# A decode block's output projection and FFN2 with activations stationary in column tiles

## The chip, the cores and the metric

One core of one Trainium2 chip runs the whole program. The metric is device time in microseconds (us) of one execution; most executions of one kernel agree within a few tenths of a microsecond, and "span" is the profiled execution from its first to its last instruction. In this text PE is TensorE (PEld its weight loads), DVE is VectorE, ACT is ScalarE, POOL is GpSimd and SP is SyncE, the engine that issues all large loads here. The page counts 16 DMA engines to the core, and the trace has 16 landings for each of the 73 large loads; I take these shares as one an engine.

## The reference

Two parallel branches share a layer-normalised token, two batch rows, one new position each:

```python
xn = layernorm(x)                                      # x: [2, 1, 512]
q = (xn @ wq)                                          # 32 heads of 128
o = softmax(q . K / sqrt(128)) . V                     # K, V: [2, 32, 8192, 128] bf16
out = x + o @ wo + relu(xn @ w1) @ w2                  # wo: [4096, 512], w1: [512, 1792]
```

K and V are 134 MB each, so nearly all of the work is reading them once.

## The kernel before

The parts that the change and the argument touch, cut. The head of PE's program, with the small FFN done while the first K tile is under way:

```python
for j in range(FJ):                                    # FJ = 14, after FFN1 and relu
    i = pe.matmul(y, lhsT=hT[:, j, :], rhs=w2_sb[:, j, :],       # [128x2] stationary, 512 moving
                  start=(j == 0), stop=(j == FJ - 1))
...
v.tensor_tensor(out=ys[:], in0=y, in1=xsb[:], op=ALU.add)        # DVE: FFN + x, [2, 512]
...
with pe.Fori(...):            # the loop over 32 tiles of K and V: transposes, scores, weighted sums
```

The tail, after the loop. The last V tile comes in two halves, wo in five pieces of 14, 7, 6, 3 and 2 of 32 slices:

```python
for k in range(KT):                                    # KT = 4: FFN + x transposed into fin, f32
    pe.matmul(fin[:, k, :], lhsT=ys[:, k * P:(k + 1) * P], rhs=ident2[:], start=(k == 0), stop=False)
...                                                    # last weighted sum, heads to OX
for c in range(NC):
    pe.wait_ge(dW[c], 16)                              # piece c of wo has landed
    for j in range(cuts[c], cuts[c + 1]):
        for k in range(KT):
            t = pe.matmul(fin[:, k, :], lhsT=wo_sb[:, j, k * P:(k + 1) * P], rhs=OX[:, j, :], ...)
...
v.tensor_copy(yT[:], fin...)                           # DVE, then
pe.transpose(tp[1][0:8, 0, :], yT[...], identb[:])     # PE, then
v.tensor_copy(osb[:], tp[1][0:8, 0, :])                # DVE
sp.dma_start(out.rearrange("b s (c p) -> (b s c) p", p=P), osb[:])   # 8 neighbouring partitions
```

## Time and profile before

| | before |
|---|---|
| time, first three runs | 660.88 us median (660.88 to 661.12) |
| span of the profiled execution | 658.7 us |
| read from HBM | 280.50 MB, 426 GB/s over the span |
| last piece of wo landed | 654.86 us |
| store issued | 656.09 us |
| store's issue to end of span | 2.57 us |

The prediction below shows the page's lines and the two timelines that matter.

### The profile page before, as it was taken

Reading aid. Unit: us, or ns where it says so; the run is one execution under the profiler, and the core shown is the slowest. Engines: PE = TensorE matmul, PEld = TensorE weight load, DVE = VectorE, ACT = ScalarE, POOL = GpSimd, SP = SyncE. Lnnn points to the kernel's source line nnn. Section 1 sums busy time; section 2 is a strip of 40 time slices with the busy share of each in tenths; the row PEclk is TensorE's granted clock in tenths of the full one; section 3 lists DMA queues with packets and bytes.
Section 4 is the critical chain, followed back from the end, with each engine's and each line's share of the span. In section 5 each row is a group of like instructions: output and inputs, shape, how many; then the busy total and the mean of one; then the engine's idle time right before and its main releaser. Section 6 shows DMA issues by size and latency. Waiting matters only on the chain.

```text
span 658.7 us, 26859 instructions
## 1 busy us (share of the span) xinstructions
PE 559.9 (85%) x12737; PEld 536.7 (81%) x12737; DVE 253.2 (38%) x436; ACT 255.8 (39%) x403; POOL 8.8 (1%) x46
## 2 busy tenths in 40 slices
PE   2897799998889978789878878987888898878897
PEld 0497798987889978789878878987888898878896
DVE  1144344443434434334433434443334443434341
ACT  1034344443433534244353434434343434433340
POOL 1000000000000000000000000000000000000000
PEclk9889999998998989899988989898899988989996
DMA  8999999999999999999999999999999999999996
GB/s 365 433 440 420 439 428 431 436 426 438 422 442 422 440 432 428 438 424 442 420 442 424 436 436 426 438 422 442 424 438 430 430 438 424 440 422 442 424 425 282
DMA packets 10542, 280.66 MB, mean 426 GB/s; under 512 B 1186, under 2 KB 1188, under 8 KB 1700
## 3 DMA queue, kind: packets, MB, share of 16 engines
q1 hardware_dynamic: 10528, 280.50, 99.1%
q8 instruction: 9, 0.15, 0.1%
q14 instruction: 1, 0.01, 0.0%
q10 hardware_dynamic: 4, 0.00, 0.0%
HBM read 280.50 MB, written 0.00 MB: 426 GB/s over the span
## 4 chain that ended last, share of the span: by engine, by line
DMA 58%; PE 37%; ACT 2%; issue 1%; SPq 1%; ACTq 0%; DVE 0%
DMA ks<-in_A_k_cache_dram 54%; PE tp L288 21%; PE Sc L295 11%; PE ot L308 4%; DMA w_sb<-in_A_wo_dram 4%; ACT kT L415 2%; ACT L415 1%; SPq L190 0%; PE Sc L343 0%; SPq L185 0%; PE Sc L346 0%; SPq L173 0%; SPq L172 0%; SPq L166 0%; PE ot L400 0%
## 5 line engine op out<-in xcount | busy, mean ns | idle before, releaser
L288 PE MATMUL tp<-identb,ks 128*128 128x128 bf16 x4096 | 323.4, 228 | 67.8 <-DMA ks<-in_A_k_cache_dram 67.8
L415 DVE COPY kT<-tp 128x1024 bf16<-128x1024 bf16 x320 | 219.7, 691 | 323.8 <-PE tp L288 323.5
L288 PEld LDWEIGHTS tp<-identb,ks 128*128 128x128 bf16 x4096 | 255.0, 102 | 71.6 <-DMA ks<-in_A_k_cache_dram 71.5
L415 ACT COPY kT<-tp 128x1024 bf16<-128x1024 bf16 x192 | 194.3, 1012 | 231.2 <-PE tp L288 231.2
L295 PE MATMUL Sc<-q,kT 128*128 128x64 bf16 x4096 | 217.1, 196 | 9.3 <-ACT kT L415 6.1
L295 PEld LDWEIGHTS Sc<-q,kT 128*128 128x128 bf16 x4096 | 178.8, 100 | 13.1 <-ACT kT L415 9.6
L308 PE MATMUL ot<-prm,vs 128*128 128x64 bf16 x4224 | 157.6, 193 | 3.3 <-issue 3.3
L308 PEld LDWEIGHTS ot<-prm,vs 128*128 128x128 bf16 x4224 | 140.5, 98 | 6.2 <-issue 3.6
L528 ACT COPY nm<-Sc 128x2 f32<-128x2 f32 x32 | 5.1, 160 | 119.8 <-PE Sc L346 119.8
L532 ACT ACTIVATE prm<-Sc,nm 64x128 bf16<-64x128 f32 x64 | 25.7, 401 | 4.4
L469 DVE TENSOR_REDUCE mcol<-Sc 64x1 bf16<-64x128 f32 x64 | 18.6, 291 | 20.0 <-PE Sc L295 19.5
L415 ACT ACT_TABLE_LOAD x16 | 20.5, 1283 | 2.2
L243 PE MATMUL ot<-vs,xz 128*16 128x512 bf16 x32 | 8.6, 436 | 8.1 <-DMA vs<-in_A_wq_dram 8.1
L474 DVE TENSOR_REDUCE mx<-Sc 1x2 bf16<-1x128 bf16 x32 | 8.9, 279 | 16.9 <-PE Sc L343 16.9
L520 ACT COPY OTf<-ot 128x2 f32 x32 | 5.1, 160 | 26.1 <-PE ot L308 26.1
L243 PEld LDWEIGHTS ot<-vs,xz 128*16 128x16 bf16 x32 | 3.1, 99 | 13.1 <-issue 10.4
L228 POOL COPY q<-qb 128x2 bf16<-128x2 bf16 x32 | 5.8, 184 | 590.1 <-PE Sc L295 568.2
L532 ACT ACTIVATION_READ_ACCUMULATOR prm<-Sc,nm x64 | 11.8, 185 | 0.0
L445 DVE TENSOR_SCALAR qs<-ot 16x512 bf16<-16x512 f32 x1 | 0.7, 678 | 16.5 <-PE ot L243 16.5
L343 PE MATMUL Sc<-identb,mcol 128*1 128x128 bf16 x32 | 7.0, 217 | 0.0
L346 PE MATMUL Sc<-mx,onesb 1*128 1x2 bf16 x32 | 5.5, 172 | 0.0
L400 PE MATMUL ot<-OX,w_sb 128*128 128x2 bf16 x128 | 4.0, 166 | 1.1 <-DMA w_sb<-in_A_wo_dram 0.7
(56 smaller groups left out, 38.0 us busy)
## 6 DMA issues: line engine op xcount, KB each, us to landing
ks<-in_A_k_cache_dram SPq DMA_DIRECT2D x32, 4096.0 KB, 26.7
vs<-in_A_v_cache_dram SPq DMA_DIRECT2D x31, 4096.0 KB, 31.3
vs<-in_A_wq_dram SPq DMA_DIRECT2D x1, 4096.0 KB, 12.1
vs<-in_A_v_cache_dram SPq DMA_DIRECT2D x2, 2048.0 KB, 19.0
w_sb<-in_B_w_dram SPq DMA_DIRECT2D x2, 1792.0 KB, 17.9
w_sb<-in_A_wo_dram SPq DMA_DIRECT2D x1, 1792.0 KB, 25.1
w_sb<-in_A_wo_dram SPq DMA_DIRECT2D x1, 896.0 KB, 26.8
w_sb<-in_A_wo_dram SPq DMA_DIRECT2D x1, 768.0 KB, 28.2
```

The costliest lines, as they stand in the source:

```text
L228: g.tensor_copy(q2[t % R][:], qb[:, 2 * t:2 * t + 2]).then_inc(sQ1, 1)
L243: i = pe.matmul(qp, lhsT=xz[:, kt, Z - g * Bsz:Z - g * Bsz + QG * Bsz], rhs=vs[1][:, (kt * QG + g) * 512:(kt * QG + g + 1) * 512], start=( ...
L288: t = pe.transpose(tp[e % 4][:, i, :], ks[r][:, kk * Dh:(kk + 1) * Dh], identb[:])
L295: t = pe.matmul(Sc[r][:, 2 * kk:2 * kk + 2 * REP], lhsT=kT[e % 4][:, i, :], rhs=rep(q2[r][:]), start=True, stop=True,)
L308: t = pe.matmul(ot[r][:, 0:2 * REP], lhsT=vs[r][:, kk * Dh:(kk + 1) * Dh], rhs=rep(prm[r][:, kk, :]), start=(kk == 0), stop=(kk == KB - 1),)
L343: pe.transpose(tr_of(r), mcol[r][:], identb[:]).then_inc(sT, 1)
L346: pe.matmul(bc_of(r), lhsT=onesb[:], rhs=mx[r][:], start=True, stop=True).then_inc(sB, 1)
L415: fn(kT[e % 4][:], tp[e % 4][:]).then_inc(kR[e], 1)
L469: m = v.tensor_reduce(out=mcol[i][half, :], in_=S_of(i)[half, :, u], axis=AX.X, op=ALU.max)
L474: v.tensor_reduce(out=mx[i][:], in_=tr_of(i).rearrange("o (u m) -> o u m", u=2), axis=AX.X, op=ALU.max, negate=True,).then_inc(sX, 1)
L520: a.copy(OTf[:, bass.ds(c, 2)], ot[r][:, 0:2]).then_inc(sO, 1)
L532: x = a.activation(out=prm[i][half, :, u], in_=S_of(i)[half, :, u], func=ACTF.Exp, bias=nm[i][half, u:u + 1], scale=1.0, accum_out=RS[half ...
```

## The change

The intent is a shorter tail. The two activations become the stationary operand, 32 columns wide with the two batch rows in columns 0 and 16 and zeros between, and the weights the moving one. The four column blocks of the result go to four column tiles of the array, partitions 32c to 32c+31. The result is then already in rows, so that one DVE add and one store of eight rows, 16 partitions apart, replace copy, transpose and copy. FFN2 takes the same form so that its rows lie where those of wo do.

```diff
-    y = Sc[1][0:Bsz, :]
-    fin = ot[0][:, 0:KT * Bsz].rearrange("p (b c) -> p c b", c=KT)
+    y = Sc[1][:, 0:P]
+    fin = ot[0][:, 0:P]
+    def cols(ap, c):
+        return ap[c * CT:(c + 1) * CT, :]              # CT = 32, CB = 16
+    def store(eng):
+        eng.dma_start(out.rearrange("b s (c p) -> c (b s) p", p=P),
+                      osb[0:P - CB + 1:CB, :]).then_inc(dO, 16)
...
         for j in range(FJ):
-            i = pe.matmul(y, lhsT=hT[:, j, :], rhs=w2_sb[:, j, :], ...)
+            for c in range(KT):
+                pe.matmul(cols(y, c), lhsT=hT[:, j, :], rhs=w2_sb[:, j, c * P:(c + 1) * P], ...)
+        for c in range(KT):
+            i = pe.matmul(cols(y, c), lhsT=onex[:], rhs=xsb[:, c * P:(c + 1) * P], ...)
...
-        for k in range(KT):
-            pe.matmul(fin[:, k, :], lhsT=ys[:, k * P:(k + 1) * P], rhs=ident2[:], ...)
...
                     t = pe.matmul(
-                        fin[:, k, :], lhsT=wo_sb[:, j, k * P:(k + 1) * P], rhs=OX[:, j, :], ...
+                        cols(fin, k), lhsT=OX[:, j, :], rhs=wo_sb[:, j, k * P:(k + 1) * P], ...
-        pe.transpose(tp[1][0:Bsz * KT, 0, :], yT[:]..., identb[:])
...
-        v.tensor_copy(yT[:], ...)
-        v.tensor_copy(osb[:], tp[1][0:Bsz * KT, 0, :])
+        v.tensor_tensor(out=osb[:], in0=fin, in1=ys[:], op=ALU.add)
```

(Zero fills and semaphore counts are left out.)

More of the change, by code (lines that the diff above doesn't have):

```diff
@@ L59 @@
     eps = 1e-5
+    CT = P // KT
+    CB = CT // Bsz
+    assert KT * Bsz * CB == P
     ctx.enter_context(tc.tile_critical(no_gpsimd_drain=True))
@@ L81 @@
     identb = sb([P, P], bf16, "identb")
-    ident2 = sb([Bsz, Bsz], f32, "ident2")
     sel = sb([H, DQ, P], bf16, "sel")
@@ L107 @@
     Ob = sb([H, Bsz, Dh], bf16, "Ob")
-    OX = sb([P, WJ, Bsz], bf16, "OX")
-    hT = sb([P, FJ, Bsz], bf16, "hT")
-    ys = sb([Bsz, D], f32, "ys")
-    yT = sb([P, Bsz, KT], bf16, "yT")
-    osb = sb([Bsz * KT, P], bf16, "osb")
+    OX = sb([P, WJ, CT], bf16, "OX")
+    hT = sb([P, FJ, CT], bf16, "hT")
+    ys = sb([P, P], f32, "ys")
+    osb = sb([P, P], bf16, "osb")
+    onex = sb([Bsz, CT], bf16, "onex")
     tp = [ps([P, EG, P], bf16, f"tp{i}") for i in range(4)]
@@ L155 @@
     hp = ot[1][:, 0:FJ * Bsz].rearrange("p (j b) -> p j b", b=Bsz)
-    y = Sc[1][0:Bsz, :]
-    fin = ot[0][:, 0:KT * Bsz].rearrange("p (b c) -> p c b", c=KT)
+    y = Sc[1][:, 0:P]
[3 more added lines that the diff above has]
+    def store(eng):
+        eng.dma_start(
+            out.rearrange("b s (c p) -> c (b s) p", p=P),
+            osb[0:P - CB + 1:CB, :],
+        ).then_inc(dO, 16)
     def load_k(t):
@@ L191, in _ @@
         sp.wait_ge(sE, 1)
-        sp.dma_start(
-            out.rearrange("b s (c p) -> (b s c) p", p=P), osb[:]
-        ).then_inc(dO, 16)
+        store(sp)
     @(lambda f: f(nc.gpsimd))
@@ L217, in _ @@
             g.wait_ge(sI, 3 + u)
-        g.memset(ident2[:], 0.0).then_inc(sG, 1)
-        g.wait_ge(sG, 5)
-        g.affine_select(
-            out=ident2[:], in_=ident2[:], compare_op=ALU.not_equal, fill=1.0,
-            base=0, pattern=[[-1, Bsz]], channel_multiplier=1,
-        ).then_inc(sI, 1)
+        g.memset(OX[:], 0.0).then_inc(sI, 1)
         g.wait_ge(sV, 100)
@@ L272, in _ @@
         for j in range(FJ):
-            i = pe.matmul(
-                y,
-                lhsT=hT[:, j, :],
-                rhs=w2_sb[:, j, :],
-                start=(j == 0),
-                stop=(j == FJ - 1),
+            for c in range(KT):
+                pe.matmul(
+                    cols(y, c),
+                    lhsT=hT[:, j, :],
+                    rhs=w2_sb[:, j, c * P:(c + 1) * P],
+                    start=(j == 0),
+                    stop=False,
+                )
+        for c in range(KT):
+            i = pe.matmul(
+                cols(y, c),
+                lhsT=onex[:],
+                rhs=xsb[:, c * P:(c + 1) * P],
+                start=False,
+                stop=True,
             )
@@ L364, in _ @@
         t.then_inc(sH, 1)
-        for k in range(KT):
-            pe.matmul(
-                fin[:, k, :],
-                lhsT=ys[:, k * P:(k + 1) * P],
-                rhs=ident2[:],
-                start=(k == 0),
-                stop=False,
-            )
         for i in range(2):
@@ L400, in _ @@
                     t = pe.matmul(
-                        fin[:, k, :],
-                        lhsT=wo_sb[:, j, k * P:(k + 1) * P],
-                        rhs=OX[:, j, :],
-                        start=False,
-                        stop=(j == WJ - 1 and k == KT - 1),
+                        cols(fin, k),
+                        lhsT=OX[:, j, :],
+                        rhs=wo_sb[:, j, k * P:(k + 1) * P],
+                        start=(j == 0),
+                        stop=(j == WJ - 1),
                     )
         t.then_inc(sH, 1)
-        pe.wait_ge(sV, 106)
-        pe.transpose(
-            tp[1][0:Bsz * KT, 0, :], yT[:].rearrange("p b c -> p (b c)"), identb[:]
-        ).then_inc(sH, 1)
     def kcopy(eng, e):
@@ L422, in _ @@
         v.memset(xz[:], 0.0).then_inc(sZ, 1)
+        v.memset(onex[:], 0.0)
+        v.memset(hT[:], 0.0).then_inc(sZ, 1)
         v.memset(prm[R - 1][:], 0.0).then_inc(sP, 1)
@@ L440, in _ @@
         v.wait_ge(sQ, 1)
+        v.wait_ge(sI, 1)
         v.wait_ge(sZ, 1)
@@ L447, in _ @@
         ).then_inc(sV, 1)
+        v.wait_ge(sZ, 2)
+        v.tensor_copy(onex[:, 0:CT:CB], identb[0:Bsz, 0:Bsz])
         v.wait_ge(sF, 1)
         v.tensor_scalar(
-            out=hT[:], in0=hp, scalar1=0.0, scalar2=None, op0=ALU.max,
+            out=hT[:, :, 0:CT:CB], in0=hp, scalar1=0.0, scalar2=None, op0=ALU.max,
         ).then_inc(sF, 1)
@@ L458, in _ @@
         v.wait_ge(sF, 3)
-        v.tensor_tensor(out=ys[:], in0=y, in1=xsb[:], op=ALU.add).then_inc(sF, 1)
+        v.tensor_copy(ys[:], y).then_inc(sF, 1)
         def pair(i, n):
@@ L500, in _ @@
         v.wait_ge(sH, 3)
+        v.wait_ge(sI, 5)
         v.tensor_copy(
-            OX[:], Sc[1][:, 0:Bsz * WJ].rearrange("p (b j) -> p j b", b=Bsz)
+            OX[:, :, 0:CT:CB], Sc[1][:, 0:Bsz * WJ].rearrange("p (b j) -> p j b", b=Bsz)
         ).then_inc(sV, 1)
         v.wait_ge(sH, 4)
-        v.tensor_copy(yT[:], ot[0][:, 0:KT * Bsz].rearrange("p (b c) -> p b c", c=KT)).then_inc(sV, 1)
-        v.wait_ge(sH, 5)
-        v.tensor_copy(osb[:], tp[1][0:Bsz * KT, 0, :]).then_inc(sE, 1)
+        v.tensor_tensor(out=osb[:], in0=fin, in1=ys[:], op=ALU.add).then_inc(sE, 1)
     @(lambda f: f(nc.scalar))
```

## The prediction

> **What bounds the kernel now.** I read the page first: the slices and the share of the chain that ended last. Columns of the first two lines are 40 equal slices of the 658.7 us span.
>
> ```profile
> DMA  8999999999999999999999999999999999999996
> GB/s 365 433 440 420 439 428 431 436 426 438 422 442 422 440 432 428 438 424 442 420 442 424 436 436 426 438 422 442 424 438 430 430 438 424 440 422 442 424 425 282
> ...
> DMA 58%; PE 37%; ACT 2%; issue 1%; SPq 1%; ACTq 0%; DVE 0%
> ```
>
> The DMA engines are at 90% or more in every slice but the first and the last, at 420 to 442 GB/s. 280.50 MB of reads at about 430 GB/s are 652 us, so all but some 7 us of the span is the stream of K, V and weights. The chain puts 37% on PE because a K load is issued when an older tile has been transposed; but such a load lands 26.7 us later and needs only about 4.19 MB / 430 GB/s = 9.8 us of transfer, so more than one other load is still ahead of it, and PE does not starve the queue. The change touches nothing inside that loop. It can act in two places only: before the first K tile (FFN2) and after the last weights have landed (wo and the output).
>
> Second, the timeline of the head, to see whether FFN2 holds anything up. Columns: start, us, engine, line, operation, tiles, count, idle time before and its releaser.
>
> ```profile
> 25.57 4.87 PE L273 MATMUL Sc<-w_sb,hT 128*2 128x512 bf16 x14
> 30.48 0.68 DVE L459 TENSOR_TENSOR ys<-Sc,xsb 2x512 f32<-2x512 f32 x1 [4.46 <-PE Sc L273]
> 32.82 2.22 PE L288 MATMUL tp<-identb,ks 128*128 128x128 bf16 x24 [2.38 <-DMA ks<-in_A_k_cache_dram]
> ```
>
> FFN2 ends at 30.44, and PE then waits 2.38 us for the first K tile. FFN2 is off the path by that much.
>
> Third, the timeline of the tail.
>
> ```profile
> 642.42 1.05 PE L366 MATMUL ot<-ident,ys 2*128 2x2 f32 x8
> ...
> 643.40 5.54 PE L308 MATMUL ot<-prm,vs 128*128 128x64 bf16 x128
> ...
> 650.46 2.35 PE L400 MATMUL ot<-OX,w_sb 128*128 128x2 bf16 x84 [0.32 <-DVE OX L501]
> 653.34 1.41 PE L400 MATMUL ot<-OX,w_sb 128*128 128x2 bf16 x36 [0.54 <-DMA w_sb<-in_A_wo_dram]
> 654.90 0.38 PE L400 MATMUL ot<-OX,w_sb 128*128 128x2 bf16 x8 [0.16 <-DMA w_sb<-in_A_wo_dram]
> 655.32 0.17 DVE L505 CAST yT<-ot 128x8 bf16<-128x8 f32 x1 [4.92 <-PE ot L400]
> 655.54 0.27 PE L409 MATMUL tp<-identb,yT 128*8 128x128 bf16 x1 [0.26 <-DVE yT L505]
> 655.85 0.21 DVE L507 COPY osb<-tp 8x128 bf16<-8x128 bf16 x1 [0.36 <-PE tp L409]
> 656.09 0.37 SPq L192 DMA_DIRECT2D out_dram<-osb  x1
> ```
>
> The reader should see three waits for wo weights (the third one, for the fourth piece, falls inside the group at 653.34). From the issue rows, the five pieces land at about 649.2 (624.15+25.1), 651.4, 653.3, 654.2 and 654.85 us. PE takes the last 8 matmuls as soon as the fifth piece lands; only what comes after 654.85 is exposed: 0.38 matmuls, then copy, transpose, copy, and the store from 656.09 to 658.70. That exposed tail is all that the change can shorten.
>
> Fourth, busy time by stretch, cut where the granted clock changes. Columns: stretch, its us, busy us and count of PE, PEld, DVE, ACT, POOL, clock, DMA share, GB/s.
>
> ```profile
> 641.03:644.44 3.41, 3.03 (x62) 2.88 (x59) 0.78 (x2) 0.16 (x1) 0.00 (x0) 1.00 1.00 423
> 644.44:647.86 3.42, 3.42 (x70) 3.42 (x67) 0.00 (x0) 0.00 (x0) 0.00 (x0) 0.50 0.97 411
> 647.86:651.27 3.41, 2.46 (x72) 2.05 (x70) 0.66 (x3) 0.00 (x0) 0.00 (x0) 1.00 0.99 405
> 651.27:654.69 3.42, 2.76 (x94) 2.56 (x91) 0.00 (x0) 0.00 (x0) 0.00 (x0) 0.50 0.66 258
> ```
>
> PE is at half clock for most of wo. Wider matmuls must be sized at that clock.
>
> [...] the store here takes 2.61 us from issue to the end of the span, and I take it as fixed.
>
> **The change, part by part.**
>
> FFN2: 14 matmuls with 512 moving columns become 56 plus 4 (x through a 0/1 stationary) with 128. At half clock and one after another they would take 60 x 0.107 = 6.4 us (0.107 is a quarter of the 0.427 us spacing of the 512-column matmuls here); start 25.57, end 32.0, still before 32.82. Four abreast they take about 60 x 0.03 = 1.8 us. Both cost nothing. The ys step (0.68 us on 512 elements per partition) becomes a 128-element copy, also hidden. The added zero fills on DVE and POOL fall in the first 5 us, while wq lands only at 13.2. Worth 0.
>
> The four f32 matmul calls (8 passes, L366) leave PE before the last V tile. From 642.42 to 643.40 that is 0.98 us, so the last weighted sum starts about 1 us sooner. Its second half needs the V half that lands at about 645.0 (623.67+21.3), so it cannot keep much more than that. wo can then begin at about 649.3, when its first piece lands, in place of 650.46. This start is slack, not time: later pieces still land when they land.
>
> wo: the same number, 128 matmuls, but stationary 128x32 and moving 128x128. Before, 84 of them took 2.27 us, 27 ns each. If four column tiles run side by side, even at half clock a group of four streams in 0.107 us, again 27 ns each. The first 84 then take 2.3 us between 649.3 and 653.3, with the wait for 651.4 inside; room is (653.3−649.3)/84 = 48 ns each. So PE again waits for the last piece. The last 8: spacing before is (0.38−0.166)/7 = 31 ns, 0.166 being one 2-column matmul in this stretch; one 128-column matmul at this clock is 0.27 us (the transpose at 655.54). So 7 x 0.031 + 0.27 = 0.49 us in place of 0.38: **+0.10 us**.
>
> After the matmuls: removed are the cast, the wait, the transpose, the wait and the copy, 655.32 to 656.06, or 0.74 us. Added is one DVE add, 128 f32 elements per partition from PSUM and SBUF. Two adds or multiplies with such operands give its size: 0.16 us for 2 elements (648.98) and 0.68 for 512 (30.48), or 1.02 ns per element; 128 elements make 0.16 + 126 x 0.00102 = 0.29 us. So **−0.74 + 0.29 = −0.45 us**.
>
> The store: eight rows of 256 bytes as before, read from partitions 16 apart in place of 8 neighbours; two KB either way, I give it 0.
>
> Sum: +0.10 − 0.45 = −0.35 us on 660.88, or 660.53. I predict 660.5.
>
> **Rivals.** (1) The column tiles do not overlap, and every matmul streams alone. [...] about 661.9. At half clock throughout it would be 128 x 0.107 = 13.7 us, ending near 663.0: about 668. For it: no trace of this case shows overlap. [...] (2) Overlap, but the 32-column loads do not hide: [...] about 661.3. The loads here have hidden so far (the wq stream at 0.427 us per 512 columns shows none of their 0.13 us). (3) The whole gain is hidden, because the store's fixed part or the spread rows eat it: 660.9. The store's landing follows its issue with nothing else in the queue, so I doubt it. (4) The earlier work at the head lets the K stream go faster: no, that queue is full.
>
> **Range and chances.** The three runs before lie within 0.24 us, so noise is about the size of the effect. Overlap with a hidden load has about 75% in my judgement and gives 660.2 to 660.8; rivals 1 and 2 share most of the rest and give 661.2 to 662. The range 660.1 to 661.4 covers the first and most of rival 2. Two per cent is 13.2 us: nothing at the head or tail is that large, save something unforeseen in the loop, so within 2% gets 0.98.
>
> **What would show it.** Right: matmuls of wo still wait for the last two pieces of wo; 8 matmuls and one DVE add of about 0.29 us stand between the last landing and the store; the store is issued near 655.7. FFN2 ends before the first K transposes. Wrong: wo with no DMA wait in it and a store issued after 656.1 (overlap absent, or loads exposed); [...] a longer issue-to-end of the store than 2.61 us; or a last wo landing that has itself moved, which would be the stream and not this change.

## More of the kernel before

One line of the page's part on DMA queues was not shown there, and turns out to be the one that counts. Its columns are packets, MB, and share of 16 engines' span:

```profile
q1 hardware_dynamic: 10528, 280.50, 99.1%
q8 instruction: 9, 0.15, 0.1%
```

The kernel's own transfers are the first line. The second is nine packets of 16 KB that the kernel never issues and that the page calls instruction: fetches of blocks of its instructions.

## The result, and the profile after

The changed kernel takes 662.28 us (662.16 to 662.64, six runs), the kernel before 661.0 us (660.82 to 661.77, six runs). The ratio of the fast runs is 1.0019, with a 95% interval of 1.0006 to 1.0032. (Ratios here are the mean time of one kernel's fast runs over the mean of the other's in the same rounds, so not quite the ratio of the medians.) That is 1.3 us slower, where 0.35 faster was predicted, and outside the range.

The page of the changed kernel, its lines for DMA and for the chain of waits, look as before (cut):

```profile
GB/s 362 435 439 424 430 433 431 437 427 433 429 433 435 429 435 425 433 439 429 435 425 433 437 429 437 425 433 435 431 437 425 433 435 431 433 427 435 431 424 242
...
q8 instruction: 9, 0.15, 0.1%
...
DMA 59%; PE 37%; ACT 2%; issue 1%; SPq 1%; ACTq 0%; DVE 0%
```

The loop is the same stream. Only the last slice differs by much, 242 GB/s against 282. The head, in the timeline of the changed kernel:

```profile
26.73 1.69 PE L278 MATMUL Sc<-w_sb,hT 128*32 128x128 bf16 x56 [0.16 <-DVE hT L455]
...
28.69 0.29 DVE L465 COPY ys<-Sc 128x128 f32<-128x128 f32 x1 [1.57 <-PE Sc L286]
...
32.86 2.74 PE L301 MATMUL tp<-identb,ks 128*128 128x128 bf16 x24 [4.22 <-DMA ks<-in_A_k_cache_dram]
```

FFN2 with 60 matmuls takes 1.9 us (26.73 to 28.63) in place of 4.87. That is 32 ns each; one after another they would have taken some 107 ns each (an estimate: a quarter of the 427 ns between the 512-column matmuls before, the granted clock being 0.50 in both). So the column tiles do run abreast, and PE waits 4.22 us for K in place of 2.38. And the tail:

```profile
649.52 1.60 PE L405 MATMUL ot<-w_sb,OX 128*32 128x128 bf16 x56 [1.05 <-DMA w_sb<-in_A_wo_dram]
...
651.62 0.94 PE L405 MATMUL ot<-w_sb,OX 128*32 128x128 bf16 x28 [0.50 <-DMA w_sb<-in_A_wo_dram]
...
653.50 0.83 PE L405 MATMUL ot<-w_sb,OX 128*32 128x128 bf16 x24 [0.95 <-DMA w_sb<-in_A_wo_dram]
...
655.74 1.04 PE L405 MATMUL ot<-w_sb,OX 128*32 128x128 bf16 x20 [1.41 <-DMA w_sb<-in_A_wo_dram]
656.38 0.14 PEld L405 LDWEIGHTS ot<-w_sb,OX 128*32 128x32 bf16 x8 [0.39 <-DMA w_sb<-in_A_wo_dram]
656.84 0.29 DVE L512 TENSOR_TENSOR osb<-ot,ys 128x128 bf16<-128x128 f32 x1 [7.91 <-PE ot L405]
657.16 0.71 SPq L166 DMA_DIRECT2D out_dram<-osb  x1
```

PE now waits for every piece of wo. The first three pieces are taken up at 649.5, 651.6 and 653.5, within 0.3 us of where they were due. The fourth is taken up at 655.74, where it was due at 654.2, and the last at 656.38, where it was due at 654.9. So PE is not late: the data is. The end of the span splits like this (us; the sum is the difference of the spans, 660.24 − 658.66):

| step | before | after | difference |
|---|---|---|---|
| last piece of wo landed | 654.86 | 656.33 | +1.47 |
| landing to start of DVE | 0.46 | 0.51 | +0.05 |
| start of DVE to issue of the store | 0.77 | 0.32 | −0.45 |
| issue of the store to end | 2.57 | 3.08 | +0.51 |
| sum | | | +1.58 |

What the change does by itself came out about as worked out, 0.40 us gained. It is more than paid back by two things: wo lands 1.47 us later, and the store takes 0.51 us longer.

The busy time by stretch tells how the landing is late. Columns: stretch, its us, busy us and count of PE, PEld, DVE, ACT, POOL, granted clock, DMA share, GB/s. Before:

```profile
653.00:654.00 1.00, 0.66 (x24) 0.66 (x24) 0.00 (x0) 0.00 (x0) 0.00 (x0) 0.50 0.50 197
654.00:655.00 1.00, 0.71 (x21) 0.55 (x18) 0.00 (x0) 0.00 (x0) 0.00 (x0) 0.50 0.19 61
```

After:

```profile
653.00:654.00 1.00, 0.50 (x20) 0.50 (x24) 0.00 (x0) 0.00 (x0) 0.00 (x0) 0.50 0.57 213
654.00:655.00 1.00, 0.34 (x16) 0.07 (x4) 0.00 (x0) 0.00 (x0) 0.00 (x0) 0.50 0.17 53
655.00:656.00 1.00, 0.26 (x12) 0.25 (x12) 0.00 (x0) 0.00 (x0) 0.00 (x0) 0.50 0.05 16
```

From 655 to 656 the sixteen engines are 5% busy: as much as one engine at 0.8 of its time with fifteen idle, and the packets below show that it is so. The whole kernel waits for one DMA engine. The trace has a record of every DMA packet, without the engine's number; these are its 16 KB instruction packets near the end and the end of the last data packets of wo (us from the span's start):

```
            8th fetch   9th fetch       last data of wo   landing of the 16 shares of the last piece, us before the last share
before      649.56      654.25          654.42            2.01 1.81 1.72 1.70 1.63 1.60 1.56 1.53 | 0.33 0.27 0.26 0.11 0.07 0.05 0.04 0.00
after       647.03      653.48-654.59   655.91            3.31 3.30 3.29 3.21 3.04 2.79 2.73 2.55 | 1.67 1.66 1.65 1.64 1.62 1.44 1.33 | 0.00
```

In the changed kernel the ninth packet runs from 653.48 to 654.59 on one engine, and behind it that engine still has two packets of the fourth piece and eight of the last; they end at 655.91, when all others have long finished. That they are on one engine is read from their times: from 654.6 on nothing else of wo is under way, and each of the ten starts within 0.03 us of the end of the one before it, the first at the end of the fetch. In the kernel before, the ninth packet starts at 654.25, and nothing of wo ends later than 654.42.

The shares of the landing show more. The engines stand in two groups of eight, some 1.5 us apart, in both kernels. The groups come into being in the head. In the kernel before, the first eight fetches start at 27.2, 43.0, 49.1, 56.1, 63.4, 69.8, 108.3 and 649.6 us; counting the shares that land within 0.5 us of the last one:

```
tile landed at, us             32.77  52.29  62.02  81.49  110.62  654.86
fetches begun until then           1      3      4      6       7       9 (the 9th 0.6 us earlier)
engines in the late group          1      3      4      6       7       8
```

So each of the first eight fetches puts one more engine about 1.5 us behind: they fall on eight different engines. The packet records show how 1.5 comes about: in the head a fetch takes 1.02 to 1.10 us, and the 32 KB packet that follows it 1.67 to 1.76 us, where the median of such packets is 1.22. From 110 to 649 us the engines are busy without a gap (DMA share 1.00), and none catches up: every landing from 110.62 to 651.40 us has seven shares in the late group and nine in the other. In the changed kernel seven engines are one step late and one is two steps late: the ninth fetch has fallen on an engine that had had one.

### The profile page after: what moved, and what is told of

Same layout as the page of the kernel before. It is cut to its first block, busy times and chain, and to the rows that moved or that the text cites. A ratio compares the mean times of both kernels' runs of the same rounds, so it can differ in the third digit from the quotient of the medians.

```text
span 660.2 us, 26934 instructions
## 1 busy us (share of the span) xinstructions
PE 557.1 (84%) x12774; PEld 535.8 (81%) x12774; DVE 254.1 (38%) x438; ACT 255.8 (39%) x403; POOL 9.5 (1%) x45
## 4 chain that ended last, share of the span: by engine, by line
DMA 59%; PE 37%; ACT 2%; issue 1%; SPq 1%; ACTq 0%; DVE 0%
DMA ks<-in_A_k_cache_dram 54%; PE tp L301 21%; PE Sc L308 11%; PE ot L321 4%; DMA w_sb<-in_A_wo_dram 4%; ACT kT L416 2%; ACT L416 1%; SPq L201 0%; PE Sc L356 0%; SPq L196 0%; PE Sc L359 0%; PE ot L405 0%; SPq L184 0%; SPq L183 0%; SPq L177 0%
## 5 line engine op out<-in xcount | busy, mean ns | idle before, releaser
L301 PE MATMUL tp<-identb,ks 128*128 128x128 bf16 x4096 | 325.4, 229 | 71.7 <-DMA ks<-in_A_k_cache_dram 71.7
L321 PEld LDWEIGHTS ot<-prm,vs 128*128 128x128 bf16 x4224 | 139.1, 97 | 5.8 <-issue 2.5
L405 PE MATMUL ot<-w_sb,OX 128*32 128x128 bf16 x128 | 4.3, 304 | 4.0 <-DMA w_sb<-in_A_wo_dram 3.9
L405 PEld LDWEIGHTS ot<-w_sb,OX 128*32 128x32 bf16 x128 | 3.0, 133 | 5.2 <-DMA w_sb<-in_A_wo_dram 4.0
```

The lines of the kernel that those rows point to most:

```text
L301: t = pe.transpose(tp[e % 4][:, i, :], ks[r][:, kk * Dh:(kk + 1) * Dh], identb[:])
L321: t = pe.matmul(ot[r][:, 0:2 * REP], lhsT=vs[r][:, kk * Dh:(kk + 1) * Dh], rhs=rep(prm[r][:, kk, :]), start=(kk == 0), stop=(kk == KB - 1),)
L405: t = pe.matmul(cols(fin, k), lhsT=OX[:, j, :], rhs=wo_sb[:, j, k * P:(k + 1) * P], start=(j == 0), stop=(j == WJ - 1),)
```

## The experiments

My theory F: the ninth fetch starts earlier, because PE's program has become longer in front of it, and it delays an engine that still holds wo. The built programs, a matmul counted as a load and a matmul, have 2331 PE instructions before and 2413 after. (f32 matmuls are counted once here, though the trace shows two passes of each; counted twice, the numbers are 2343 and 2417, and the order of the kernels below hardly changes.) Rival C: reading wo as moving operand in column tiles slows its landing. For the store: either the 16 partitions between its rows (theory S), or the permuted order in the result (theory D).

The first two pads, the third of the same kind, and a store with other rows. The pad stands after FFN2 in PE's program and is idle work:

```diff
+        for _ in range(90):                            # 38 and 64 in the others
+            pe.matmul(ot[1][:, 508:510], lhsT=identb[:], rhs=identb[:, 0:2], start=True, stop=True)
```

**after_pad90.** 

> The changed kernel with 90 idle matmul pairs (a stationary load and a 2-column matmul into unused PSUM columns) after FFN2, where PE waits over 4 us for the first K tile anyway. Theory F (fetch): the 1.3 us come from a 16 KB instruction fetch of PE that occupies one DMA engine for 1.1 us while that engine still holds packets of the last two wo pieces; where it falls depends on how many instructions PE has passed. [...] the fetch is back where it was in the kernel before: the last wo piece lands near 654.9 in place of 656.3, and the time is about 660.9 (my 660.5 plus the 0.45 that the store itself has become longer). Rival C (column tiles): PE's reading of the weights as moving operand slows the landing of the last pieces; then pads do nothing and the time stays at 662.3.

Measured 662.29 us (662.06 to 662.5) against 660.81 before: expectation missed. The profile says why. The longer program has one fetch more, ten in place of nine, of which eight fall into the head; the ninth starts at 650.43 and the tenth at 654.28. It is the ninth that puts one engine two steps behind, as in the changed kernel (its shares of the last piece: eight at 3.07 to 3.45 us, seven at 1.41 to 1.75, one at 0). What must not come early is the ninth fetch of the program, wherever in the code it is. Of my expectation only this came true: a fetch, the tenth, starts at 654.28, where one, the ninth, started at 654.25 in the kernel before.

**before_pad38** (the same with 38, in the kernel before). 

> The kernel before with 38 idle matmul pairs after FFN2 (about 1 us, inside the 2.4 us that PE waits there), nothing else changed. Theory F: the fetch now falls where it falls in the changed kernel, cuts into the last wo pieces, and the time rises by about 1.3 us to 662.2, with the last wo landing near 656.3. Rival C: this kernel has no column tiles, so it stays at 660.9 to 661.1.

Measured 662.0, 662.17, 660.75, 660.9 and 660.92 us: two levels of one kernel, 1.2 us apart, half as expected. The profiled execution is the one of 662.0. In it the ninth fetch starts at 653.79, wo's data ends at 655.75, and one engine is 1.29 us behind the next. There is no column tile in this kernel, so rival C cannot explain the upper level; but at this length the fetch seems to come just at the edge.

**after_pad64.** 

> As after_pad90 with 64 pairs. Theory F: the second fetch of the tail now falls some 26 pairs later than in the kernel before, at the end of wo or after it, so it delays nothing: last wo landing near 654.8, time 660.8 to 660.9, not above after_pad90. If the fetch matters only by its number and not by its place, this equals the changed kernel, 662.3. Rival C: 662.3.

Measured 714.82 us, six runs between 695.87 and 717.65, which I had not expected. Four of the six, the profiled one of 714.88 among them, count as slow; the two fast ones, 695.87 and 702.65, are 1.058 of the kernel before (interval 1.054 to 1.062), or 38 us slower. How much of the wider spread is the fetches' own isn't known. The lines of its page on bandwidth, on the instruction queue and on the K transposes:

```profile
GB/s 367 438 427 435 427 430 429 315 425 434 429 378 384 390 412 423 282 382 439 432 417 363 399 413 430 421 263 431 423 434 416 331 435 425 425 294 425 422 339 227
...
q8 instruction: 72, 1.18, 0.7%
...
L306 PE MATMUL tp<-identb,ks 128*128 128x128 bf16 x4096 | 320.8, 227 | 102.6 <-issue 99.1
```

There are 72 fetches of 16 KB in place of 9, nine in every stretch of 82 to 88 us all through the loop, and PE stood 99.1 us before its transposes with nothing to wait for that the profile shows ("issue"), where the idle time there in the changed kernel, 71.7 us, is all for K. What is shown is that 64 pads bring the fetches into the loop, where 90 do not. Why they do is not shown: no run here tries the neighbouring counts. This run says nothing about theory F.

**after_rows0to7.** `osb[0:P - CB + 1:CB, :]` became `osb[0:KT * Bsz, :]`. Its output is wrong, which doesn't matter for the time. 

> The changed kernel whose store reads partitions 0 to 7 in place of 0, 16, ..., 112: the result is wrong on purpose. Theory S (source stride): the store's issue falls from 0.71 to about 0.37 us and issue to end from 3.05 to about 2.6, so the time is about 661.8. Rival D (destination order): the order of the rows in the result is what costs; then nothing changes, 662.3. The last wo landing stays late (near 656.3) in both.

Measured 662.27 us (661.19 to 663.37), unclear as a time. The issue in the profile, however, is plain, and theory S falls:

```profile
658.12 0.80 SPq L166 DMA_DIRECT2D out_dram<-osb  x1
```

The profiled execution was the slowest of the five. In it the engines fell apart by another microsecond at about 90 us, when nine packets of 32 KB took 1.5 to 3.0 us in place of 1.2 with no fetch among them, for a reason that I could not find (it is left open below); single runs of other kernels, the kernel before among them (661.77), lie about 1 us high as well.

The second group was to settle rival C and the store.

**after_oldffn2.** The changed kernel with FFN2 as before, then four small matmuls that spread the two rows to their partitions; wo, add and store stay as changed.

```diff
+            i = pe.matmul(Sc[1][0:Bsz, :], lhsT=hT[:, j, 0:CT:CB], rhs=w2_sb[:, j, :], ...)
...
+            i = pe.matmul(cols(ot[1][:, 0:P], c), lhsT=onex[:], rhs=ys0[:, c * P:(c + 1) * P], ...)   # f32
```

> The changed kernel with the FFN2 of the kernel before (14 matmuls of 512 columns; x added on DVE; 4 small matmuls then spread the rows), so wo in column tiles, the one add and the one store stay. PE's program has 2329 instructions, against 2413 in the changed kernel and 2331 in the kernel before. Theory F, as the first four runs left it: each instruction fetch of 16 KB delays one DMA engine by some 1.3 us, the first eight fall on eight different engines, the ninth on one of them again; it harms if it starts while that engine still has wo packets. Here the ninth should start near 654.3, as in the kernel before, and harm nothing: last wo landing near 654.9, time near 660.9 to 661.0 (660.5 as predicted plus 0.45 for the longer store). Rival C (reading wo as moving operand of column tiles delays its landing): wo is unchanged, so 662.3.

Measured 660.7, 660.74, 660.96, 661.03 and once 662.65 us; before 660.86. The median, 660.96, is where theory F put it and 1.3 under the changed kernel, though wo is untouched. Rival C falls. (The profile fell on the run of 662.65, which has a disturbance of the kind just told, at about 70 us, so its lines are not used.)

**before_pad80** (80 idle pairs in the kernel before). 

> The kernel before with 80 idle matmul pairs after FFN2 (about 2.3 us, about what PE waits there), 2491 PE instructions. Theory F: the ninth fetch starts some 40 pairs earlier in wo than in before_pad38, at about 650 to 652 us, where its engine always has wo packets left; so all runs are slow, near 662.2, the last wo landing near 656.3. Rival C, or any reason that lies in the column tiles: 660.9. If before_pad38's two levels (660.8 and 662.1) were chance alone, this shows two levels again.

Measured 662.18 us (661.93 to 662.27, and one of 663.32), before 660.86 (660.73 to 661.66); the ratio is 1.0018, interval 1.0004 to 1.0031. The kernel before, lengthened by hidden work alone (after the pads PE still waits 0.60 us for the first K tile), is now at the upper level in every run. The timeline of its tail has the very picture of the changed kernel, in the old form of wo:

```profile
653.47 0.75 PE L405 MATMUL ot<-OX,w_sb 128*128 128x2 bf16 x24 [0.64 <-DMA w_sb<-in_A_wo_dram]
...
655.96 0.48 PE L405 MATMUL ot<-OX,w_sb 128*128 128x2 bf16 x12 [1.74 <-DMA w_sb<-in_A_wo_dram]
...
657.77 0.37 SPq L192 DMA_DIRECT2D out_dram<-osb  x1
```

Here too PE waits 1.7 us for the fourth piece. The ninth fetch starts at 653.69, not at 650 to 652 as I had expected. So the start does not simply move with the count of instructions; in these profiles it tends to come near the time when PE goes on after a wait for wo (fetch at 653.69 and PE at 653.47 here, 653.48 and 653.50 in the changed kernel, 654.25 and 654.26 in the kernel before), which is not tested further.

**after_ffn1short.** Only the length goes back: 14 of FFN1's 56 matmuls are left, FFN2 and wo stay in column tiles. Its output is wrong, which doesn't matter for the time.

```diff
-            for kt in range(KT):
+            for kt in range(1):
```

> The changed kernel, FFN2 in column tiles, wo and store as they are, but with 14 of the 56 matmuls of FFN1 (one of four slices of the contraction; wrong on purpose). FFN1 is hidden work before the first K tile, like FFN2. Only the length of PE's program goes back: 2329 instructions, as in after_oldffn2, 84 less than in the changed kernel. Theory F (length of the program places the ninth fetch): most runs near 660.9 to 661.0, last wo landing near 655.0. If it were FFN2's column tiles themselves and not the length: 662.3.

Measured 661.11 us (660.9 to 662.11), before 660.92. Four of five runs lie at 660.9 to 661.34. The ninth fetch starts at 654.48 and wo has landed at 655.01:

```profile
654.32 0.25 PEld L405 LDWEIGHTS ot<-w_sb,OX 128*32 128x32 bf16 x12 [0.35 <-DMA w_sb<-in_A_wo_dram]
...
655.05 0.41 PE L405 MATMUL ot<-w_sb,OX 128*32 128x128 bf16 x8 [0.22 <-DMA w_sb<-in_A_wo_dram]
```

The fourth and the last piece are taken up at 654.32 and 655.05, as in the kernel before. So it is neither FFN2's column tiles nor wo's, but the number of instructions in front. The number does not settle every run: at this length one of five (662.11) lies at the upper level, and in after_inorder, as long as the changed kernel, one of five (661.12) at the lower.

Over all profiles but three (after_rows0to7 and after_oldffn2 with the other disturbance, after_pad64 with its 72 fetches), the start of the ninth fetch sorts the last landing without an exception: up to 653.84 it is late, from 654.25 on it is not.

| kernel | PE instructions | 9th fetch starts, us | last wo landing, us | profiled run, us |
|---|---|---|---|---|
| after_pad90 | 2593 | 650.43 | 656.42 | 662.35 |
| after | 2413 | 653.48 | 656.33 | 662.31 |
| before_pad80 | 2491 | 653.69 | 656.54 | 663.32 |
| before_pad38 | 2407 | 653.79 | 656.16 | 662.0 |
| after_inorder | 2413 | 653.84 | 656.47 | 662.17 |
| before | 2331 | 654.25 | 654.86 | 660.79 |
| oldffn2_plainstore | 2329 | 654.33 | 655.00 | 660.59 |
| after_ffn1short | 2329 | 654.48 | 655.01 | 661.11 |
| before_permstore | 2331 | 654.53 | 655.06 | 661.5 |
| oldffn2_2stores | 2329 | 654.64 | 655.20 | 661.19 |

(The time also holds the store, which is longer in some of these. The 663.32 of before_pad80 has a span of 660.3 us, as the others of the upper half; its extra microsecond lies outside the span.)

The store, next. **after_inorder** stores its rows 16 partitions apart as they come, in the order of the result, `"b s (c p) -> (b s c) p"`. Its output is wrong, which doesn't matter for the time. 

> The changed kernel whose store writes its eight rows in the order of the result (batch, column block) though they lie in the order column block, batch: the result is wrong on purpose. Theory D: issue about 0.37 us in place of 0.71, and from issue to end of span about 2.6 in place of 3.05; time about 661.85. If source partitions 16 apart were what costs (after_rows0to7 speaks against it: its issue took 0.80 us), nothing changes: 662.3. The late landing of wo stays in both.

Measured 662.17 us (661.12 to 662.35). The issue did not become short:

```profile
657.29 0.73 SPq L166 DMA_DIRECT2D out_dram<-osb  x1
```

So neither cause alone is the one: theory D falls as S did. **oldffn2_2stores** has one store for each batch row, on SP and ACT, from partitions 32 apart:

```diff
+        eng.dma_start(out.rearrange("b s (c p) -> (b s) c p", p=P)[b],
+                      osb[b * CB:P - CT + b * CB + 1:CT, :])      # b = 0 on SP, b = 1 on ACT
```

> As after_oldffn2, with two stores in place of the one: SP stores batch row 0 from partitions 0, 32, 64, 96, ACT row 1 from 16, 48, 80, 112; each has its rows in the order of the result. Theory D (the permuted order of the destination makes the store's issue 0.71 us long and its data 0.5 us late): each issue about 0.4 us, issue to end about 2.6, time about 660.5, so 0.4 under after_oldffn2. If the cost is in something else, about equal to after_oldffn2.

Measured 661.14 us (660.83 to 661.22), a little above after_oldffn2's fast runs; the issues take 0.67 and 0.60 us, and the end comes 3.3 us after them. A miss: if the partitions count too, neither of the two is plain.

The built program has a hint: the store of the kernel before carries a mark in it that those of after_inorder, after_rows0to7 and the changed kernel do not have. Theory P is that the short issue needs both sides plain: neighbouring partitions, and the result in order.

**oldffn2_plainstore.** after_oldffn2 with the store of the kernel before, from partitions 0 to 7 in order. 

> As after_oldffn2, but the store is word for word that of the kernel before: partitions 0 to 7, written in the order of the result (wrong on purpose). Theory P (the short issue of 0.37 us needs both a source of neighbouring partitions and a destination in order; either one missing makes it 0.7 to 0.8 us): issue 0.37, issue to end about 2.6, time about 660.5, that is 0.45 under the fast runs of after_oldffn2, and just what was predicted for the change. If the longer store comes from something else in the changed tail (the wide add just before it), issue stays 0.71 and the time 660.9.

Measured 660.48 us (660.18 to 660.7), before 660.85 (660.74 to 661.32). Its tail:

```profile
654.42 1.03 PE L407 MATMUL ot<-w_sb,OX 128*32 128x128 bf16 x20 [0.29 <-DMA w_sb<-in_A_wo_dram]
655.50 0.29 DVE L516 TENSOR_TENSOR osb<-ot,ys 128x128 bf16<-128x128 f32 x1 [6.11 <-PE ot L407]
655.82 0.37 SPq L167 DMA_DIRECT2D out_dram<-osb  x1
```

The issue is 0.37 us again, and the end comes at 658.4, 2.6 us after it. With the fetch and the store as before, what is left of the change is worth 660.48 − 660.85 = −0.37 us by the medians, which is what was predicted, though the interval of the ratio (0.9979 to 1.0007) does not exclude none. It is no kernel to use, as its result is wrong.

**before_permstore.** The kernel before with only the order of its store permuted. Its output is wrong, which doesn't matter for the time. 

> The kernel before, its eight rows stored in the permuted order (column block, batch) to the result, the source unchanged: wrong on purpose. Theory P: issue 0.7 to 0.8 us, issue to end about 3.05, time about 661.3. If the store's length depends on the changed tail: 660.85.

Measured 661.5 us (661.36 to 661.83), +0.65 by the medians (interval of the ratio 0.9996 to 1.0023; the issue, though, is clear). Theory P holds both ways, and the size was rather too small:

```profile
656.29 0.79 SPq L192 DMA_DIRECT2D out_dram<-osb  x1
```

Whether the form costs by itself, or through the mark, stays open: in every run the store with the mark has the short issue and those without it the long one, so no run parts the two.

No version that gives the right result beats the kernel before. The nearest, after_oldffn2 and oldffn2_2stores, come to the same time within noise: what they gain before the store they lose in it.

## Why the prediction was wrong, point by point

**What bounds the kernel** was right: the stream, and at the end the last landing of wo. **The column tiles** were right and better than worked out: the last 8 matmuls took about 0.43 us in place of 0.49 (landing to DVE grew by 0.05 us, not 0.10), the first 56 took 1.60, and PE waited for the last pieces in every profile. Rivals 1 and 2, tiles that do not overlap or loads that do not hide, did not occur. (That the tiles would overlap was my guess, and the 661.9 and 661.3 of these rivals were my estimates: no trace of the kernel before shows them.) **The tail after the matmuls** was right: the one add took 0.29 us, as worked out, and the step gained 0.45.

**The step that failed** is in two sentences: FFN2's "Both cost nothing. … Worth 0" and, of the wo phase, "later pieces still land when they land". They took work that PE hides to be free, and the landing of a transfer to depend on the transfers alone. The runs show in its place that the length of PE's program shifts the moment when its next block of instructions is fetched (653.48 us in place of 654.25), that the fetch takes one DMA engine out of the stream for 1.1 us, and that a landing waits for the slowest of sixteen: wo landed 1.47 us later. FFN2's 46 more matmul pairs cost no time where they stand, and about 1.3 us at the end, 620 us later. This is shown from both sides: the kernel before became as slow by length alone (before_pad80, +1.3), and the changed kernel lost the delay by length alone (after_ffn1short, −1.2 against the changed kernel's median).

**A mis-sized term** is "either way, I give it 0" for the store. It measured +0.51 us in the changed kernel: a third of a microsecond of longer issue (0.71 for 0.37) and the rest on the way to the data. The prediction took the store as fixed, at 2.61 us (2.57 by the span). By the trace's semaphore records only the part from issue to landing varies, 1.20 us before and 1.72 after; the 1.37 us from there to the end are the same in both. The cause was not only the one I looked at, the 16 partitions between the rows; either departure from the plain form is enough.

With those two terms the sum closes: 660.53 + 1.3 + 0.5 = 662.3, and 662.28 was measured. That it closes so well is partly luck: in the two profiles the late landing alone is 1.47.

**The rivals.** Rival 3, that the store eats the gain, was half true: it ate the gain (0.51 for 0.40), but that leaves the larger part of the loss unexplained. The last point of the list of signs named the right one, "a last wo landing that has itself moved", but dismissed it as "the stream and not this change". It was the stream, moved by this change.

**The range** held only what overlap and load hiding could do. It had no room for an effect on the end from work in the head.

What stays open: why the first eight fetches fall on eight different engines and the ninth on one of them; what exactly starts the ninth fetch; and what the rarer disturbance of about 1 us is, which moved single runs of several kernels, the kernel before among them.

## What to carry to other kernels

Where a kernel ends on the last landing of a stream that keeps all DMA engines full (a DMA share of 1.00 from 110 to 649 us here), look for the fetches of its instructions too: in these runs each was a transfer of 16 KB that held one engine for 1.02 to 1.11 us in the profiles before and after, those in the head put one engine each about 1.5 us behind, and hidden work that added instructions moved the ninth to where it was exposed, at a cost of about 1.3 us. Compare versions on the same side of such a step before judging what a change is worth, and check the page's count of instruction packets whenever a loop's code moves; 9 became 72 with a pad of 64 matmuls, and the two fast runs of that were 38 us slower. And look at the form of an end-of-kernel store before trading compute for it: half a microsecond of the gain went there. In these runs its issue took 0.37 us from neighbouring partitions to the result in order, and 0.60 to 0.80 us with either one otherwise; the end of the span came 2.5 to 2.6 us after the start of the issue in the first form and 3.1 to 3.3 us in the others.
